# Attention and a gated feed-forward layer: outer weight units by chunk, weights split on GpSimd and copies on ScalarE in batch 0, end rows paired off chip

## The chip, the cores and the metric

One core of a Trainium2 chip runs the kernel. Its engines are TensorE (PE, matmuls; the loading of its weights is shown as PEld), VectorE (DVE), ScalarE (ACT), GpSimd (POOL) and the DMA queue of SyncE (SP); the time is that of one execution on the device, in microseconds (us). A change counts as measured when it is over about 0.2%.

## What is computed

Attention with a soft cap on the scores for 4 batches of 12 heads, 448 rows of 64, and behind it a gated product with 1536 inner columns:

```python
scores = cap * tanh(q @ k.T / sqrt(64) / cap)
x = softmax(scores) @ v             # (4, 12, 448, 64) -> x of (1792, 768)
gate = 1 / (1 + exp(-(x @ w_gate)))  # w_gate, w_val of (768, 1536)
out = (gate * (x @ w_val)) @ w_out   # w_out of (1536, 768)
```

Everything is in 32 bits; the three weights come in 64 bits.

## The kernel before

**Precision.** Each product of the feed-forward layer is made of three matmuls: an operand is split into a high part (a copy rounded to the type that TensorE takes, `hi`, line 207 on POOL, 209 on ACT, 211 on DVE) and a low part (the difference, `lo`, line 215), and the products high x low, high x high and low x high are added up in PSUM.

**Staging.** The attention runs in 24 steps of two heads (`_bounded_attention`), six to a batch. The feed-forward layer of a batch is `moe(b)`: a first product (24 units of weights, gate and value columns in turn, 18 matmuls of 448 columns a unit, line 893), and a second product (12 units, six for each half `t` of the output columns, line 984). The second product has the 384 full rows of the batch as 3 chunks of 128; a unit is 2 of the 12 inner blocks (`KU`), so 6 matmuls of 384 columns for each chunk, 18 for a unit. The 64 rows left in each batch (`REST`) go to DRAM (`grest`) and are gathered for the last batch, which works them as two more chunks of 128. While `moe(b)` runs, the attention of batch b + 1 is put between its matmuls; the two generators are advanced in turn by the amounts that they yield. Before that the attention of batch 0 runs alone, to about 70 us. By the trace batch 0 of the layer takes from 72 to 262 us, batch 1 to 431, batch 2 to 596, and batch 3, with no attention beside it, to the end.

**Order.** The orders of TensorE and ACT are those in which the program is written. Those of DVE, POOL and SP are made by the scheduler from priorities and a timeline of its own, and are then fixed; `tc.high_priority` moves an instruction ahead.

**Weights.** There are 36 units in a batch. In batch 0 they come in 64 bits (line 752) into three buffers, are converted to 32 bits by ACT (line 769) and three steps of DVE (lines 770 to 772) into one of two `pair` buffers, and are split into one of four `wspl` buffers (`WB = 4`): the high part by ACT and the low part by DVE, but for the first four units both by POOL (`o.early = 4`). `next_w(u)`, called just before the matmuls of unit u, converts unit u + 4, splits unit u + 3 (`AHEAD`) and hands out unit u. Split units are stored in DRAM (`wd`, line 822) and loaded again in the batches behind (`load_to(u + WB)`, line 843, into the slot that unit u - 1 has left); twelve units of a batch (`whole`) are stored as 32 bits (`wr`, line 779) and split on chip each time. The first four units are stored from ACT's queue when they are used.

**PSUM.** The feed-forward layer has three tiles (tag `m`), which both products go round in. ACT's tanh (line 934) reads a gate tile, DVE (line 937) a value tile, POOL and DVE split the result (`gspl`); the second product's tiles are copied to SBUF with a factor 0.5 (line 1006 on DVE, 1008 on ACT) and go out from SP's queue (line 1011). In batches 0 to 2 all copies are DVE's; in batch 3 DVE and ACT take turns.

## Time and profile before

| | |
|---|---|
| median of three runs | 756.18 us (755.86 to 757.0) |
| profiled execution | 755.29 us, span 753.5 us |
| PE busy | 739.8 us, 3900 matmuls |
| PEld, DVE, ACT, POOL busy | 639.7, 506.5, 378.2, 217.1 us |
| mean granted TensorE clock | 0.997 of full speed |
| matmuls of the first product | 377.2 us |
| matmuls of the second product | 159.6 us on a batch's own rows, 26.6 on the gathered ones |
| DMA | 151.78 MB, mean 201 GB/s |

An engine's busy time is the time in which any of its instructions runs. A row of an instruction begins with its start and length in us; in square brackets stands how long its engine was idle before it and what ended that. A row of waits has the engine and line that waited, what it waited for, the sum in us, the times and the longest.

### The profile page before, as it was taken

The numbers are of one execution on the slowest core, as the hardware profiler recorded it, in microseconds if no ns is written. First come the engines' busy times: TensorE is split into PE (matmuls) and PEld (weight loads), VectorE is DVE, ScalarE is ACT, GpSimd is POOL, SyncE is SP. The second block draws the span as 40 slices with busy tenths as digits, with TensorE's granted clock in tenths as the row PEclk, the third lists the DMA queues.
The fourth block names the chain that finished last, engine by engine and source line by source line (L and its number), as shares of the span: only waits on it lengthen the run. The fifth ranks groups of instructions, "written<-read, shape, count | busy, mean of one in ns | idle before, by whom it ended". The sixth has DMA issues, their size and how long they took to land.

```text
span 753.5 us, 10326 instructions
## 1 busy us (share of the span) xinstructions
PE 739.8 (98%) x3900; PEld 639.7 (85%) x3900; DVE 506.5 (67%) x544; ACT 378.2 (50%) x418; POOL 217.1 (29%) x223
## 2 busy tenths in 40 slices
PE   8999999999999999999999999999999999999996
PEld 6556777777788888888899988988989999999996
DVE  2898688979999939988897638889877132322000
ACT  5997577767577346666564246665561011111000
POOL 1364001021211616463545305455552000000000
PEclk9999999999999999999999999999999999999998
DMA  5866898997899964444567954523379946463541
GB/s 125 224 151 157 294 324 249 319 282 257 259 266 383 310 200 150 106 157 134 165 185 247 296 166 151 142 102 113 126 195 308 335 152 187 148 194 99 184 159 57
DMA packets 133511, 151.78 MB, mean 201 GB/s; under 512 B 86860, under 2 KB 111948, under 8 KB 133452
## 3 DMA queue, kind: packets, MB, share of 16 engines
q1 hardware_dynamic: 130588, 147.02, 63.1%
q10 hardware_dynamic: 2864, 4.00, 1.5%
q8 instruction: 33, 0.54, 0.3%
q14 instruction: 26, 0.21, 0.1%
HBM read 118.75 MB, written 31.46 MB: 199 GB/s over the span
## 4 chain that ended last, share of the span: by engine, by line
PE 82%; DVE 8%; DMA 3%; issue 2%; POOL 2%; ACT 1%; SPq 1%; ACTq 0%; POOLq 0%; DVEq 0%
PE h L893 43%; PE o L984 20%; PE sc L413 6%; PE pv L474 4%; PE pv L484 2%; PE pv L483 2%; DVE rd L530 2%; DVE pair L772 1%; PE tp L244 1%; PE pv L465 1%; DVE pair L771 1%; DMA qk<-in_k_dram 1%; PE tp L360 1%; DMA wd<-wspl 1%; DMA wspl<-wd 1%
## 5 line engine op out<-in xcount | busy, mean ns | idle before, releaser
L893 PE MATMUL h<-xspl,wspl 128*128 128x448 f32 x1728 | 377.2, 372 | 0.9 <-DVE osb L1006 0.9
L893 PEld LDWEIGHTS h<-xspl,wspl 128*128 128x128 f32 x1728 | 321.3, 188 | 42.7 <-issue 15.2
L984 PE MATMUL o<-wspl,gspl 128*128 128x384 f32 x864 | 159.6, 338 | 1.4 <-DVE gate L937 1.2
L984 PEld LDWEIGHTS o<-wspl,gspl 128*128 128x128 f32 x864 | 150.4, 188 | 6.4 <-issue 3.8
L207 POOL TENSOR_SCALAR gspl<-gate 128x448 fp32r<-128x448 f32 x48 | 42.8, 891 | 240.8 <-DVE gate L937 240.4
L416 ACT ACTIVATE t<-sc,scale 128x896 f32<-128x896 f32 (+1 forms) x90 | 85.9, 1002 | 32.2 <-PE sc L413 31.9
L209 ACT ACTIVATE wspl<-pair 128x768 fp32r<-128x768 f32 x68 | 57.5, 845 | 87.4 <-PE h L893 72.7
L937 DVE SCALAR_TENSOR_TENSOR gate<-gate,h 128x448 f32<-128x448 f32 x48 | 29.7, 618 | 84.8 <-PE h L893 70.3
L424 ACT ACTIVATE t<-t,capv 128x1792 f32<-128x1792 f32 (+2 forms) x48 | 83.3, 1738 | 0.8 <-issue 0.6
L215 DVE TENSOR_TENSOR wspl<-pair,wspl 128x768 fp32r<-128x768 f32 x68 | 74.5, 1095 | 3.3 <-ACT wspl L209 2.9
L530 DVE RECIPROCAL rd<-rd 128x448 f32<-128x448 f32 x24 | 70.7, 2947 | 5.5 <-ACT rd L503 2.7
L934 ACT ACTIVATE gate<-h 128x448 f32<-128x448 f32 x48 | 26.0, 543 | 92.0 <-PE h L893 91.3
L413 PE MATMUL sc<-T 64*128 64x448 f32 (+1 forms) x522 | 66.5, 382 | 1.1 <-DVE T L215 1.1
L413 PEld LDWEIGHTS sc<-T 64*128 64x128 f32 (+1 forms) x522 | 44.9, 181 | 20.7 <-issue 12.1
L1006 DVE TENSOR_SCALAR osb<-o 128x384 f32<-128x384 f32 x22 | 11.9, 554 | 61.0 <-PE o L984 60.9
L436 POOL TENSOR_TENSOR a<-t 128x448 f32<-128x448 f32 x24 | 31.7, 1323 | 70.3 <-ACT t L424 37.4
L209 ACT ACTIVATE ph<-t 128x1792 fp32r<-128x1792 f32 x24 | 40.8, 1699 | 14.5 <-PE pv L485 14.4
L215 DVE TENSOR_TENSOR pl<-t,ph 128x1344 fp32r<-128x1344 f32 x24 | 47.2, 1968 | 0.4
L215 DVE TENSOR_TENSOR gspl<-gate,gspl 128x448 fp32r<-128x448 f32 x48 | 38.5, 802 | 7.7 <-POOL gspl L207 7.4
L769 ACT ACTIVATE pair<-w 128x768 f32<-128x768 f32 x36 | 32.5, 907 | 19.1 <-DVE wspl L215 10.5
L772 DVE SCALAR_TENSOR_TENSOR pair<-w,pair 128x768 uint16<-128x768 uint32 x36 | 41.8, 1165 | 0.3
L474 PE MATMUL pv<-t,vo 112*128 112x448 f32 x96 | 40.1, 539 | 0.4 <-ACT t L424 0.4
(92 smaller groups left out, 721.4 us busy)
## 6 DMA issues: line engine op xcount, KB each, us to landing
wspl<-wd SPq DMA_DIRECT2D x72, 768.0 KB, 5.7
wd<-wspl SPq DMA_DIRECT2D x20, 768.0 KB, 5.3
pair<-wr SPq DMA_DIRECT2D x36, 384.0 KB, 3.1
w<-in_moe_w_gate_dram SPq DMA_DIRECT2D x12, 768.0 KB, 6.8
w<-in_moe_w_val_dram SPq DMA_DIRECT2D x12, 768.0 KB, 6.7
w<-in_moe_w_out_dram SPq DMA_DIRECT2D x12, 768.0 KB, 6.9
qk<-in_q_dram SPq DMA_DIRECT2D x44, 112.0 KB, 4.7
wr<-pair SPq DMA_DIRECT2D x12, 384.0 KB, 3.8
```

The source lines that it names most:

```text
L207: self.nc.gpsimd.tensor_scalar(dst, src, 1.0, 1.0, ALU.mult, ALU.mult)
L209: self.nc.scalar.activation(dst, src, AF.Copy)
L215: e.tensor_sub(dst, src, hi.bitcast(F32))
L413: nc.tensor.matmul(ps[0:w, j, 0:S], a[rows], r[rows], start=(i == 0), stop=(i == len(ops) - 1))
L416: nc.scalar.activation(Pt[n][0:w, :, m, :], ps[0:w, :, 0:S], AF.Tanh, scale=c["scale"][0:w])
L424: nc.scalar.activation(t, t, AF.Exp, scale=c["cap"][rows])
L474: nc.tensor.matmul(pv, vs[n][0:QC, j * NC + m, :], Pt[n][0:QC, j, m, :], start=(m == 0), stop=(m == NC - 1),)
L530: nc.vector.reciprocal(rd, rd)
L769: nc.scalar.activation(x, top.bitcast(F32), AF.Copy, scale=2.0 ** -112)
L772: nc.vector.scalar_tensor_tensor(half, low.bitcast(U32), 2.0 ** -29, half, ALU.mult, ALU.add)
L893: nc.tensor.matmul(ps, a, r, start=(kk == 0 and i == 0), stop=(kk == KD - 1 and i == 2))
L984: nc.tensor.matmul(ps, a, r, start=(y + kk == 0 and i == 0), stop=(y + kk == KF - 1 and i == 2),)
```

## The change

The high part of the weights goes from ACT to POOL for all units of batch 0 (`u < NU`), not the first four alone. Units 0 to 2 are stored in DRAM already in the attention steps 4 to 6 (`store_early`). The output copies are written behind each chunk (`copy_out`) and no longer behind all chunks; in batch 0 they are ACT's. In batches 1 and 2 the first two and the last two units of each half of the second product are worked together: for each chunk the matmuls of both units, then the next chunk; what prepares the units to come, for the second of the two, stands behind both. And the end rows of two batches lie beside each other in DRAM (`grest` of 128 columns), and the tiles that they are gathered in have those 128 columns innermost.

```diff
@@ -558,6 +558,8 @@
         live, last = n < NP, n == o.NPAIR
         if live:
             due = emit_S(n, 0) + emit_S(n, 1)
+            if NC <= n <= o.NPAIR:
+                o.store_early(n - NC)
             if n in PLAN:
                 o.convert_to(PLAN[n])
             yield due
@@ -809,7 +811,7 @@
         if u not in w_raw:
             return
         t, s = w_raw.pop(u), new_w(u)
-        o.hi("p" if u < o.early else "a", s[:, 0, :], t)
+        o.hi("p" if u < NU else "a", s[:, 0, :], t)
         o.lo("p" if u < o.early else "v", s[:, 1, :], t, s[:, 0, :])
         if u < KEEP or u >= o.early:
             w_spl[u] = s
@@ -870,18 +872,23 @@
 
     R, NR, KR = o.REST, B * o.REST, 3
     assert NR % P == 0
-    g_rest = []
-
-    def next_w(u):
+    g_rest, GR = [], P // R
+
+    def prepare_w(u):
         if u < NU:
             convert_to(u + LEAD)
         split_w(u + AHEAD)
         load_to(u + WB)
         load_raw_to(u + LEAD + 2)
-        w = w_spl.pop(u)
-        if u < KEEP:
-            store_w(u, w, nc.scalar)
-        return w
+
+    def store_early(u):
+        if u < KEEP and u not in w_dram:
+            store_w(u, w_spl[u], nc.scalar)
+
+    def next_w(u):
+        prepare_w(u)
+        store_early(u)
+        return w_spl.pop(u)
 
     def moe(b):
         u0 = b * NU
@@ -901,14 +908,16 @@
         if b == B - 1:
             tiles = []
             for tag, bufs, n in o.rest_tags:
-                r = ap.tile([P, n, 2, KR, NR], F32R, tag=tag, bufs=bufs, name=f"rest{len(tiles)}")
+                r = ap.tile([P, n, 2, NR // P, KR, P], F32R, tag=tag, bufs=bufs, name=f"rest{len(tiles)}")
                 tiles += [r[:, i] for i in range(n)]
             for x, r in enumerate(tiles):
-                for bb, d in enumerate(g_rest):
-                    nc.sync.dma_start(
-                        out=r[:, :, :, bb * R:(bb + 1) * R].bitcast(F32),
-                        in_=d[:, :, x * KR:(x + 1) * KR, :].bitcast(F32),
-                    )
+                for at, d in enumerate(g_rest):
+                    n = P if at < b // GR else b % GR * R
+                    for i in (range(2) if n < P else [slice(0, 2)]):
+                        nc.sync.dma_start(
+                            out=r[:, i, at, :, 0:n].bitcast(F32),
+                            in_=d[:, i, x * KR:(x + 1) * KR, 0:n].bitcast(F32),
+                        )
                 rest.append(r)
         u = u0
 
@@ -945,18 +954,21 @@
             lambda i, k, at=m * P: g_spl[:, i, k, at:at + P] for m in range(o.NF)
         ]
         if b < B - 1:
-            d = dram.tile([P, 2, KF, R], F32R, name=f"grest{b}")
-            nc.sync.dma_start(out=d.bitcast(F32), in_=g_spl[:, :, :, rest_cols].bitcast(F32))
-            g_rest.append(d)
+            if b % GR == 0:
+                g_rest.append(dram.tile([P, 2, KF, P], F32R, name=f"grest{b}"))
+            nc.sync.dma_start(
+                out=g_rest[-1][:, :, :, b % GR * R:(b % GR + 1) * R].bitcast(F32),
+                in_=g_spl[:, :, :, rest_cols].bitcast(F32),
+            )
         else:
             for x, r in enumerate(rest):
                 for i in range(2):
                     nc.sync.dma_start(
-                        out=r[:, i, :, b * R:].bitcast(F32),
+                        out=r[:, i, b // GR, :, b % GR * R:].bitcast(F32),
                         in_=g_spl[:, i, x * KR:(x + 1) * KR, rest_cols].bitcast(F32),
                     )
-            for at in range(0, NR, P):
-                chunks.append(lambda i, k, at=at: rest[k // KR][:, i, k % KR, at:at + P])
+            for at in range(NR // P):
+                chunks.append(lambda i, k, at=at: rest[k // KR][:, i, at, k % KR, :])
 
 
         for t in range(2):
@@ -966,16 +978,48 @@
                     acc.append(ps_m.tile([P, HM], F32, tag="m", name=f"o{b}_{t}_{m}"))
                 else:
                     acc.append(o.two_banks(f"o{b}_{t}_{m}")[:, 0, 0:HM])
+            dst_t = out[:, t * HM:(t + 1) * HM]
+            osr = None
             end = b == B - 1 and t == 1
+
+            def copy_out(m, ps):
+                nonlocal osr
+                if m == o.NF:
+                    tag, bufs = o.out_tag
+                    osr = ap.tile([P, NR // P, HM], F32, tag=tag, bufs=bufs, name=f"osr{b}_{t}")
+                if m < o.NF:
+                    dst = big.tile([P, HM], F32, tag="gate", bufs=3, name=f"osb{b}_{t}_{m}")
+                else:
+                    dst = osr[:, m - o.NF, :]
+                if end and m == len(acc) - 1:
+
+                    hm = HM // 2
+                    nc.vector.tensor_scalar(dst[:, 0:hm], ps[:, 0:hm], 0.5, None, ALU.mult)
+                    nc.scalar.activation(dst[:, hm:], ps[:, hm:], AF.Copy, scale=0.5)
+                elif m % 2 == 0 and b > 0 or 0 < b < B - 1:
+
+                    with tc.high_priority(offset=2 * AHEAD_OF):
+                        nc.vector.tensor_scalar(dst, ps, 0.5, None, ALU.mult)
+                else:
+                    nc.scalar.activation(dst, ps, AF.Copy, scale=0.5)
+                if m < o.NF:
+                    at = b * S + m * P
+                    nc.sync.dma_start(out=dst_t[at:at + P], in_=dst)
+
             by_chunk = KF - CLOSE * KU if end else KF
             x = 0
             while x < KF:
                 units = []
-                for y in range(x, KF if x >= by_chunk else x + KU, KU):
-                    units.append((y, next_w(u)))
+                if x >= by_chunk:
+                    to = KF
+                elif 0 < b < B - 1 and x in (0, KF - 2 * KU):
+                    to = x + 2 * KU
+                else:
+                    to = x + KU
+                for y in range(x, to, KU):
+                    units.append((y, next_w(u) if y == x or end else w_spl.pop(u)))
                     u += 1
-                x += len(units) * KU
-                for ps, g_of in zip(acc, chunks):
+                for m, (ps, g_of) in enumerate(zip(acc, chunks)):
                     for y, w in units:
                         for kk in range(KU):
                             wh, wl = (w[:, i, kk * HM:(kk + 1) * HM] for i in range(2))
@@ -985,32 +1029,14 @@
                                     ps, a, r, start=(y + kk == 0 and i == 0),
                                     stop=(y + kk == KF - 1 and i == 2),
                                 )
-                    yield 3 * KU * HM / S
-            to = out[:, t * HM:(t + 1) * HM]
-            for m, ps in enumerate(acc):
-                if m == o.NF:
-                    tag, bufs = o.out_tag
-                    osr = ap.tile([P, NR // P, HM], F32, tag=tag, bufs=bufs, name=f"osr{b}_{t}")
-                if m < o.NF:
-                    dst = big.tile([P, HM], F32, tag="gate", bufs=3, name=f"osb{b}_{t}_{m}")
-                else:
-                    dst = osr[:, m - o.NF, :]
-                if end and m == len(acc) - 1:
-
-                    hm = HM // 2
-                    nc.vector.tensor_scalar(dst[:, 0:hm], ps[:, 0:hm], 0.5, None, ALU.mult)
-                    nc.scalar.activation(dst[:, hm:], ps[:, hm:], AF.Copy, scale=0.5)
-                elif m % 2 == 0 or b < B - 1:
-
-                    with tc.high_priority(offset=2 * AHEAD_OF):
-                        nc.vector.tensor_scalar(dst, ps, 0.5, None, ALU.mult)
-                else:
-                    nc.scalar.activation(dst, ps, AF.Copy, scale=0.5)
-                if m < o.NF:
-                    at = b * S + m * P
-                    nc.sync.dma_start(out=to[at:at + P], in_=dst)
+                    if to == KF:
+                        copy_out(m, ps)
+                    yield 3 * (to - x) * HM / S
+                if to > x + KU and not end:
+                    prepare_w(u - 1)
+                x = to
             if b == B - 1:
-                ends = to.rearrange("(b s) e -> b s e", s=S)[:, o.FULL:]
+                ends = dst_t.rearrange("(b s) e -> b s e", s=S)[:, o.FULL:]
                 for bb in range(B):
                     m, r = divmod(bb * R, P)
                     queue = nc.scalar if t == 1 and bb == B - 1 else nc.sync
@@ -1019,7 +1045,7 @@
 
     MS = {mybir.EngineType.PE, mybir.EngineType.Activation}
     att = attention_of(o, x_done)
-    o.convert_to, o.load_weights = convert_to, begin_w64
+    o.convert_to, o.load_weights, o.store_early = convert_to, begin_w64, store_early
     first = big.tile([1, 1], F32, name="first")
     nc.scalar.activation(first, c["ident"][0:1, 0:1], AF.Tanh)
     with tc.manual_schedule(engines=MS):
```

## Rows read from the trace of the kernel before

**Rows 1.** The page: busy us (share of the span) and instructions of each engine.

```profile
PE 739.8 (98%) x3900; PEld 639.7 (85%) x3900; DVE 506.5 (67%) x544; ACT 378.2 (50%) x418; POOL 217.1 (29%) x223
```

**Rows 2.** The waits of TensorE from 60 to 600 us.

```profile
PE o L984 <- DVE gate L937: 1.2, 1, 1.2
PE tp L360 <- ACT t L416: 1.0, 1, 1.0
PE h L893 <- DVE osb L1006: 0.9, 1, 0.9
...
PE pv L474 <- ACT t L424: 0.4, 1, 0.4
...
PE o L984 <- DVE osb L1006: 0.2, 1, 0.2
```

**Rows 3.** Window: busy (x) of PE, PEld, DVE, ACT, POOL; clock, DMA share, GB/s.

```profile
70.00:262.00 192.00, 189.43 (x962) 154.35 (x958) 167.46 (x191) 127.93 (x150) 35.54 (x32) 1.00 0.91 292
```

**Rows 4.** The timeline of ACT, early in batch 0.

```profile
84.75 0.85 ACT L209 ACTIVATE wspl<-pair 128x768 fp32r<-128x768 f32 x1 [2.69 <-PE h L893]
...
85.50 3.46 ACT L424 ACTIVATE t<-t,capv 112x1792 f32<-112x1792 f32 x2
```

**Rows 5.** The timeline of ACT, where batch 0's second product begins.

```profile
209.00 0.85 ACT L209 ACTIVATE wspl<-pair 128x768 fp32r<-128x768 f32 x1 [3.06 <-DVE pair L772]
```

**Rows 6.** The timelines of ACT and DVE, where batch 0 ends.

```profile
260.94 1.91 ACT L416 ACTIVATE t<-sc,scale 128x896 f32<-128x896 f32 x2 [9.00 <-PE sc L413]
...
261.76 1.01 DVE L1006 TENSOR_SCALAR osb<-o 128x384 f32<-128x384 f32 x2
```

**Rows 7.** The timelines of DVE and PE, where batch 2's second product begins.

```profile
554.61 0.61 DVE L937 SCALAR_TENSOR_TENSOR gate<-gate,h 128x448 f32<-128x448 f32 x1
...
551.78 2.27 PE L984 MATMUL o<-wspl,gspl 128*128 128x384 f32 x12
555.28 2.38 PE L984 MATMUL o<-wspl,gspl 128*128 128x384 f32 x12 [1.23 <-DVE gate L937]
```

**Rows 8.** High parts of weights: ACT's (ns min/median/max) to 262 us, POOL's (mean).

```profile
L209 ACT ACTIVATE wspl<-pair x32: 830/847/862, 79.3 to 247.6; 128x768 fp32r<-128x768 f32 x32
...
L207 POOL TENSOR_SCALAR wspl<-pair 128x768 fp32r<-128x768 f32 x4 | 3.3, 834 | 4.0 <-DVE pair L772 4.0
```

**Rows 9.** The timelines of POOL and DVE in batch 0, splits that meet.

```profile
202.42 1.77 POOL L207 TENSOR_SCALAR xspl<-xraw 128x448 fp32r<-128x448 f32 x2
...
203.68 1.31 DVE L215 TENSOR_TENSOR wspl<-pair,wspl 128x768 fp32r<-128x768 f32 x1
...
173.24 2.21 POOL L207 TENSOR_SCALAR gspl<-gate 128x448 fp32r<-128x448 f32 x1 [8.85 <-DVE gate L937]
```

**Rows 10.** Timelines of POOL, DVE, SP and PE at the end of batch 0.

```profile
248.55 2.35 POOL L438 TENSOR_TENSOR a<-a,t 64x448 f32<-64x448 f32 x1
...
251.41 0.96 DVE L215 TENSOR_TENSOR wspl<-pair,wspl 128x768 fp32r<-128x768 f32 x1
252.29 2.95 DVE L530 RECIPROCAL rd<-rd 128x448 f32<-128x448 f32 x1
...
252.82 0.38 SPq L843 DMA_DIRECT2D wspl<-wd  x1
...
251.78 8.31 PE L984 MATMUL o<-wspl,gspl 128*128 128x384 f32 x47
```

**Rows 11.** DMA issues at 695 to 728, 392.6, 562 us: median us to landing.

```profile
wspl<-wd SPq DMA_DIRECT2D x7, 768.0 KB, 4.3
...
wspl<-wd SPq DMA_DIRECT2D x2, 768.0 KB, 6.1
...
wspl<-wd SPq DMA_DIRECT2D x2, 768.0 KB, 7.4
```

**Rows 12.** The timelines of SP and PE, late in batch 2's second product.

```profile
576.39 2.19 SPq L1011 DMA_DIRECT2D out_dram<-osb  x1
...
579.29 16.81 PE L984 MATMUL o<-wspl,gspl 128*128 128x384 f32 x96
```

More of the change, by code (lines that the diff above doesn't have):

```diff
@@ L968, in moe @@
                     acc.append(o.two_banks(f"o{b}_{t}_{m}")[:, 0, 0:HM])
+            dst_t = out[:, t * HM:(t + 1) * HM]
+            osr = None
             end = b == B - 1 and t == 1
-            by_chunk = KF - CLOSE * KU if end else KF
-            x = 0
-            while x < KF:
-                units = []
-                for y in range(x, KF if x >= by_chunk else x + KU, KU):
-                    units.append((y, next_w(u)))
-                    u += 1
-                x += len(units) * KU
-                for ps, g_of in zip(acc, chunks):
-                    for y, w in units:
-                        for kk in range(KU):
-                            wh, wl = (w[:, i, kk * HM:(kk + 1) * HM] for i in range(2))
-                            gh, gl = (g_of(i, y + kk) for i in range(2))
-                            for i, (a, r) in enumerate(((gh, wl), (gh, wh), (gl, wh))):
-                                nc.tensor.matmul(
-                                    ps, a, r, start=(y + kk == 0 and i == 0),
-                                    stop=(y + kk == KF - 1 and i == 2),
-                                )
-                    yield 3 * KU * HM / S
-            to = out[:, t * HM:(t + 1) * HM]
-            for m, ps in enumerate(acc):
+            def copy_out(m, ps):
+                nonlocal osr
                 if m == o.NF:
@@ L1010, in moe @@
                     at = b * S + m * P
-                    nc.sync.dma_start(out=to[at:at + P], in_=dst)
+                    nc.sync.dma_start(out=dst_t[at:at + P], in_=dst)
+            by_chunk = KF - CLOSE * KU if end else KF
+            x = 0
+            while x < KF:
+                units = []
+                if x >= by_chunk:
[6 more added lines that the diff above has]
+                    units.append((y, next_w(u) if y == x or end else w_spl.pop(u)))
+                    u += 1
+                for m, (ps, g_of) in enumerate(zip(acc, chunks)):
+                    for y, w in units:
+                        for kk in range(KU):
+                            wh, wl = (w[:, i, kk * HM:(kk + 1) * HM] for i in range(2))
+                            gh, gl = (g_of(i, y + kk) for i in range(2))
+                            for i, (a, r) in enumerate(((gh, wl), (gh, wh), (gl, wh))):
+                                nc.tensor.matmul(
+                                    ps, a, r, start=(y + kk == 0 and i == 0),
+                                    stop=(y + kk == KF - 1 and i == 2),
+                                )
+                    if to == KF:
[4 more added lines that the diff above has]
+                x = to
             if b == B - 1:
-                ends = to.rearrange("(b s) e -> b s e", s=S)[:, o.FULL:]
+                ends = dst_t.rearrange("(b s) e -> b s e", s=S)[:, o.FULL:]
                 for bb in range(B):
```

## The prediction

> **What bounds the kernel now.** I read the page's busy times first: TensorE (PE) is busy for 98% of the span [rows 1], so the span is nearly the sum of its matmuls, and the change takes none away. A matmul that waits for nothing runs at its pace, and 96 of the second product's stand in 16.81 us, 0.175 us each [rows 12]. So a gain can only come out of TensorE's waits, and the second view is the list of those, from 60 us (the attention head of batch 0 is over soon after) to 600 us (the last attention is over). It names five waits that the change could touch: 1.2 us for a gate of VectorE (DVE), 1.0 for a tanh of ScalarE (ACT), 0.9 and 0.2 for output copies on DVE, 0.4 for an exp on ACT [rows 2]. Together 3.7 us. Behind 600 us there is no such wait, and the first 60 us are not touched. That is the ceiling: 3.7 us of 755, if nothing new is late.
>
> **The change part by part.**
>
> **High parts of the weights, ACT to GpSimd (POOL), 32 instructions in batch 0.** ACT loses 32 x 0.847 us = 27 us, POOL gets 32 x 0.834 = 26.7 us [rows 8]; neither engine is full (128 and 36 us busy of 192 from 70 to 262 us) [rows 3], so the sums are worth nothing by themselves. What counts is that ACT runs in a fixed order and that this step sits in it, waiting for a weight slot or for a conversion. At 84.75 us it had waited 2.69 us for TensorE, and the exp that TensorE needed came out only at 85.5 [rows 4]: the 0.4 us. At 209.0 it had waited 3.06 us for DVE's conversion, and the tanh that frees a PSUM tile for the transposes stood behind it [rows 5]: the 1.0 us. With the step gone ACT reaches both early enough; next late would be ACT's conversion step, which waits for a pair buffer. I take both, 1.4 us.
>
> The price is on DVE. Where POOL reads SBUF beside a DVE step with two SBUF inputs, one of them is longer: the low part of a weight took 1.31 us at 203.68 beside POOL's splits [rows 9] where it takes 0.96 undisturbed [rows 10], 0.35 more; elsewhere POOL waited, its split of 448 columns lasting 2.21 us [rows 9]. A move costs DVE between 0 (POOL waits) and 0.834 us (the whole instruction). From 70 to 262 us DVE is busy 167.46 of 192 us [rows 3], so 24.5 are free, and the six copies that go to ACT free 6 x 0.55 = 3.3 more (two in 1.01 us) [rows 6]. Even 32 x 0.834 = 26.7 us stays below 27.8. I take 0.25 a move, 8 us in all (between the two rows, nearer to the one where POOL waits, because a split is released by DVE's own step and DVE goes straight on). It is covered as long as a weight is split three units before TensorE comes to it: 192 us for 36 units makes about 5 us a unit, so some 10 us.
>
> The rule in question is the Trainium skill's, "SBUF — State Buffer", section "Who interferes with whom": a DVE instruction with two SBUF inputs and a GpSimd instruction that reads SBUF exclude each other, and the second to start is held until the first is done. The trace agrees (0.35 us on DVE, or 2.21 us on POOL). Taken to its end the rule speaks against the move: every split would hold up somebody, and if it were always DVE the 24.5 us of room would be gone.
>
> Where the cover is thin is the end of batch 0. POOL is in the three adds of the attention until 248.55 + 2.35 = 250.9 us; the last unit's low part ran at 251.41, a reciprocal of 2.95 us right behind it, and the load of the next batch's first unit was issued at 252.82, behind the store that waits for that low part [rows 10]. TensorE needs that unit's low part 18 matmuls before the end of the 47 that end at 260.0, at 256.8 [rows 10]: 4.4 us of cover. A split behind the adds on POOL ends at 250.9 + 0.83 = 251.7, so the low part is done by 252.7 if DVE keeps its order: 0.3 us later, covered. The next batch's load then moves by 0.3 us as well. I book 0.3 and keep 0 to 2.2 (the rival below).
>
> **Output copies of batch 0 to ACT.** TensorE's 0.9 us at 262 is a PSUM tile whose copy DVE did only at 261.76, while ACT had been idle for 9.0 us before 260.94 [rows 6]. On ACT it is done when the matmuls end, and 0.85 + 0.2 us go. Against it: a copy now waits in ACT's order for its chunk and holds up what is behind it. That is a tanh or exp for matmuls that come later on TensorE too; and an exp of 1.8 us (two took 3.46 [rows 4]) ahead of the copy could bring back the 0.2 us. I book 1.1, between 0.8 and 1.1.
>
> **Two units by chunk at both ends of the second product, batches 1 and 2.** At 551.78 the first unit begins; the third chunk's PSUM tile was freed by the gate at 554.61 + 0.61 = 555.2, and TensorE came to it early, after 12 matmuls, and went on at 555.28 [rows 7]. With two units by chunk it comes after 24, 24 x 0.175 = 4.2 us, at 556.0. The 1.2 us go. At the other end the copies get more time, which no wait of these batches asks for.
>
> The price: both units are read until the last chunk, so their two slots come free together, and the units that refill them are asked for 36 matmuls, 36 x 0.175 = 6.3 us later, where before it was nine chunks, 9.4 us. A load took 4.3 us in quiet (7 of them), 6.1 us where two were issued together, 7.4 us beside the attention's last traffic and the gathering of the end rows [rows 11]. Besides, the queue of SP is in order: one issue of a copy took 2.19 us in this stretch instead of 0.34 or so [rows 12]. Between the two ends, -2.0 (in time) and +1.1 us late per place, the middle is on time by 0.2. There are four places without attention work between the matmuls (the second half, batches 1 and 2). I book 0.5 us in all, 0 to 6.3.
>
> **End rows paired off chip.** Twelve gathering loads stay twelve; by the shapes, four of them now move runs of 1536 bytes and eight half the bytes in runs of 256, where all were 256 on the side of SBUF. The tiles are read only in batch 3's second product, and no wait of TensorE names them [rows 2]. Nothing by itself; less traffic beside the loads above, which is why I take 0.5 there. **Three stores issued earlier** on ACT's queue, in the last attention steps before the first product: no instruction more; the bytes move out of a crowded stretch (DMA share 0.91 from 70 to 262 [rows 3]). Nothing, with 0.5 either way.
>
> **The sum.** 1.4 + 1.1 + 1.2 = 3.7 gained, 0.3 + 0.5 new: 2.9 less. The profiled execution took 755.29 us (span 753.5, 1.8 around it), so 752.4; the median of the runs, 756.18, lies 0.9 above it, so 753.3.
>
> **Rivals.** *POOL and DVE eat it at the end of batch 0.* If DVE's fixed order puts the reciprocal before the last low part: 251.7 + 2.95 + 0.96 = 255.6, the store, the load at 256.0, landing 6.1 later at 262.1. TensorE, 0.85 + 1.6 us earlier than before, would want it at 259.9 and wait 2.2 us. Left are 2.9 + 0.3 - 2.2 = 1.0: 755.2. For it: the thin cover, DVE full there; against: 251.41 shows the low part first. This is also where the skill's rule would bite first. *DVE saturated over all of batch 0* needs more than 0.87 us a move, above the whole instruction; it is out as an average.
>
> *Weights late (slower).* If each of the four places is late by the 1.1 us of the slow loads, and one issue by 1.9 more, TensorE waits 6.3 us for 3.7 gained less the 0.3: 759.1. It decides from 3.4 us on, about 0.85 a place, a landing 7.2 us behind the free slot. For it: 7.4 us was seen in just this stretch; against: 6.1 with two together, and fewer small packets.
>
> *The waits move.* The waits are short, and what was 0.3 us behind them (a conversion, a transposed tile, a copy behind an exp) takes their place: half the gain stays, 754.7 at most; the change does what it says and TensorE waits for someone else.
>
> **How the numbers follow.** Forecast 753.3, chance 0.52, own range 752 to 754.6. Rival at the end of batch 0: 0.15. Moved waits: 0.2, 754.5 to 756.5. Weights late: 0.13, 757 to 760. A measurement of this kernel tells about 0.2%, 1.5 us, from no change: faster is below 754.7. Faster: the forecast and a quarter to a half of the two middle cases, 0.64; same 0.25; slower 0.11. Range 751.8 to 757.2: below, the ceiling of 3.7 and 0.5 for the stores; above, a part of the late weights.
>
> **What would show it.** Right: of TensorE's waits from 60 to 600 us those for ACT's exp and tanh, the gate and the copies gone; the splits of weights on POOL at 0.83 to 2 us; ACT's copies right behind their chunks at 235 and 260. Wrong: waits of TensorE for loads of weights in the second halves of batches 1 and 2, or at the first unit of batch 1; DVE busy all through 230 to 262 with steps of 1.3 us and more where 0.96 stood; a first product of batch 1 that begins no earlier than 262.

## The result and the profile after

The changed kernel took 761.22 us (median of 8 runs, 759.2 to 762.51) beside 756.19 us for the one before: a ratio of 1.0057 with a 95% interval of [1.0047, 1.0068], so slower: by 5.0 us in the medians, by 4.3 as the ratio has it. The prediction was 753.3 us, faster, and its range ended at 757.2: wrong in sign and range. The profiled execution took 760.87 us, span 759.1. Below, "before" and "after" are the two kernels.

The page of after, engines (as [rows 1]):

```profile
PE 742.4 (98%) x3900; PEld 642.1 (85%) x3900; DVE 510.0 (67%) x538; ACT 356.1 (47%) x392; POOL 248.3 (33%) x255
```

The span is 5.6 us longer. 2.6 of it is *busy* time of TensorE, with the same 3900 matmuls; the other 3.0 is idle time. The waits of TensorE from 60 to 600 us in after (as [rows 2]):

```profile
PE o L1028 <- DVE wspl L215: 3.9, 1, 3.9
PE o L1028 <- DMA wspl<-wd: 1.8, 2, 1.3
PE o L1028 <- DVE gate L946: 0.6, 1, 0.6
PE tp L244 <- ACT t L416: 0.5, 1, 0.5
PE sc L413 <- DVE T L215: 0.2, 1, 0.2
```

All five waits of [rows 2] are gone, 3.7 us. In their place stand one wait of 3.9 us for a weight's low part, two for loaded weights (1.8), and one for a gate (0.6). The last two lines were there before. Two windows of after (us, then busy of PE, PEld, DVE, ACT, POOL, granted clock, DMA share, GB/s):

```profile
70.00:262.00 192.00, 187.04 (x943) 153.05 (x940) 172.13 (x186) 101.94 (x119) 62.26 (x61) 0.99 0.84 267
...
259.00:266.00 7.00, 6.28 (x24) 6.01 (x26) 2.54 (x4) 1.47 (x3) 0.56 (x1) 0.58 0.79 278
```

Beside [rows 3], ACT has 26 us less, POOL 26.7 more, and DVE 4.7 more although the copies left it. The second window is where the 2.6 us of longer matmuls are. The end of batch 0, timelines of PE, POOL and DVE in after (as [rows 10]), and last the same conversion step of DVE in before:

```profile
249.75 6.06 PE L1028 MATMUL o<-wspl,gspl 128*128 128x384 f32 x34
259.72 5.72 PE L1028 MATMUL o<-wspl,gspl 128*128 128x384 f32 x18 [3.91 <-DVE wspl L215]
...
248.27 1.74 POOL L437 TENSOR_TENSOR a<-a,t 128x448 f32<-128x448 f32 x1
250.09 1.75 POOL L438 TENSOR_TENSOR a<-a,t 64x448 f32<-64x448 f32 x1
252.89 1.98 POOL L207 TENSOR_SCALAR wspl<-pair 128x768 fp32r<-128x768 f32 x1 [1.06 <-PE o L1028]
...
244.63 1.04 DVE L774 SCALAR_TENSOR_TENSOR pair<-w,pair 128x768 uint16<-128x768 uint32 x1
...
250.86 1.89 DVE L774 SCALAR_TENSOR_TENSOR pair<-w,pair 128x768 uint16<-128x768 uint32 x1
...
254.21 1.13 DVE L215 TENSOR_TENSOR ph<-t,ph 64x448 fp32r<-64x448 f32 x1
...
255.92 2.94 DVE L530 RECIPROCAL rd<-rd 128x448 f32<-128x448 f32 x1
258.78 0.89 DVE L215 TENSOR_TENSOR wspl<-pair,wspl 128x768 fp32r<-128x768 f32 x1
...
245.62 1.86 DVE L772 SCALAR_TENSOR_TENSOR pair<-w,pair 128x768 uint16<-128x768 uint32 x1
```

Read it backwards. TensorE had done 34 matmuls by 255.8 and then stood 3.9 us for the last unit's low part, which DVE gave at 258.78 + 0.89 = 259.7. Before, it was ready at 252.4 [rows 10]. Ahead of it stood a reciprocal of 2.9 us, which came *behind* it in [rows 10]; ahead of that the last conversion, which ended at 250.86 + 1.89 = 252.75, in before at 245.62 + 1.86 = 247.48, 5.3 us earlier. It released POOL's split at 252.89 (the row names TensorE; but the slot that the split writes was that of unit 31, whose matmuls were over by 246, so it was the pair buffer that came last). Steps of DVE took 1.9 us beside POOL's adds where 1.04 stands without them; being later, three such steps on weights fell beside the adds instead of one (in before the attention's step `pl`, behind that one, was the long one: 2.51 us, against 1.55 in after). And the 18 matmuls behind the wait took 5.7 us, not 18 x 0.175 = 3.15: the granted clock in the window from 259 to 266 is 0.58, and from 258.0 to 264.8 the trace has half, the 1.2 GHz of the two levels. That is the 2.6 us of busy time.

The wait needs both, the late conversion and the new order. An estimate from these rows: in the old order the low part would have come behind the step `ph`, at 254.21 + 1.13 = 255.34 (POOL's split had ended at 252.89 + 1.98 = 254.87), and have been done at 256.3, 0.5 us after TensorE came for it instead of 3.9. No run forces the old order.

Why was the conversion late? The timelines of ACT's and SP's queues in after, 32 us earlier, and the time to landing of one of SP's issues (the columns are those of [rows 11]):

```profile
221.87 0.54 ACT L505 ACTIVATE xraw<-pv 64x448 f32<-64x448 f32 x1
224.87 0.46 ACTq L156 DMA_DIRECT2D v<-in_v_dram  x1
227.45 1.32 ACTq L161 DMA_DIRECT2D v<-in_v_dram  x2
228.82 1.80 ACT L424 ACTIVATE t<-t,capv 112x1792 f32<-112x1792 f32 x1 [6.41 <-issue]
...
219.06 0.56 SPq L824 DMA_DIRECT2D wd<-wspl  x1
219.72 0.37 SPq L754 DMA_DIRECT2D w<-in_moe_w_out_dram  x1
...
wd<-wspl SPq DMA_DIRECT2D x1, 768.0 KB, 5.8
```

ACT did nothing for 6.4 us with work at hand. It was to issue the loads of v, three transfers, and an issue waits in ACT's own order. Each transfer of this program counts its landing on a semaphore, and each of these issues of v waits until the earlier transfer on its semaphore has landed. The trace names the semaphores: in this stretch ten of them, 100 to 109, go round over the queues of SP and ACT. The first v load waits for 108, which had last belonged to the weight store issued at 219.06; that landed at 224.85, and the load went out at 224.87. The second waits for 109, which had belonged to the weight load of 219.72; that landed at 227.43, and the issue went out at 227.45. In the kernel before the scheduler had put SP's transfers in another sequence. Small loads of k had 108 and 109 and had landed by 220.83; only the third issue waited for a weight store (landed at 222.71, issue at 222.73). The same point of ACT's timeline has no gap:

```profile
221.49 0.42 ACTq L156 DMA_DIRECT2D v<-in_v_dram  x1
...
223.51 1.79 ACT L424 ACTIVATE t<-t,capv 112x1792 f32<-112x1792 f32 x1
```

Behind the gap stood an exp and a tanh of the attention and ACT's next conversion step (232.29 us); unit 32's conversion ended at 236.3, before at 232.5, and from there the conversions ended 3.3 to 3.8 us later, the last one 5.3. DVE's largest wait from 70 to 262 us, in before and then in after:

```profile
DVE pair L770 <- ACT pair L769: 14.5, 15, 2.3
...
DVE wspl L215 <- POOL wspl L207: 12.5, 12, 2.9
```

Before, DVE waited for ACT's conversion steps; after, for POOL's splits, whose low part stands next in its order. The sum is hardly different: more than half of DVE's idle time is time in which it waits in its order for a neighbour, and that part has only changed the neighbour.

Last, batch 2's second half, timelines of PE and of SP's queue in after:

```profile
588.16 7.58 PE L1028 MATMUL o<-wspl,gspl 128*128 128x384 f32 x42 [1.30 <-DMA wspl<-wd]
596.22 2.03 PE L1028 MATMUL o<-wspl,gspl 128*128 128x384 f32 x10 [0.49 <-DMA wspl<-wd]
...
582.16 3.72 SPq L917 DMA_DIRECT2D rest<-grest  x3
585.98 9.06 SPq L845 DMA_DIRECT2D wspl<-wd  x4
```

The loads for two units come out of SP's queue behind the gathering of the end rows, and TensorE waits for both.

So the ledger of the 5.6 us: -3.7 (the waits removed), +3.9 (low part), +2.6 (half clock behind it), +1.8 (loads), +0.6 (gate) make 5.2; 0.4 lies in small idle times outside these rows.

### The profile page after: what moved, and what is told of

Its sections match the earlier page's. It is cut to its first block, busy times and chain, and to the rows that moved or that the text cites. A ratio compares the mean times of both kernels' runs of the same rounds, so it can differ in the third digit from the quotient of the medians.

```text
span 759.1 us, 10351 instructions
## 1 busy us (share of the span) xinstructions
PE 742.4 (98%) x3900; PEld 642.1 (85%) x3900; DVE 510.0 (67%) x538; ACT 356.1 (47%) x392; POOL 248.3 (33%) x255
## 4 chain that ended last, share of the span: by engine, by line
PE 63%; DMA 2%; DVE 1%; SPq 0%; issue 0%; ACT 0%
PE h L900 35%; PE o L1028 17%; PE sc L413 4%; DMA wspl<-wd 2%; PE pv L484 2%; PE pv L483 2%; PE dn L522 1%; PE pv L485 1%; PE tp L360 1%; PE tp L244 1%; DVE rd L530 0%; SPq L845 0%; DVE ph L215 0%; DVE wspl L215 0%; DVE a L440 0%
## 5 line engine op out<-in xcount | busy, mean ns | idle before, releaser
L1028 PE MATMUL o<-wspl,gspl 128*128 128x384 f32 x864 | 162.8, 342 | 6.3 <-DVE wspl L215 3.9
L1028 PEld LDWEIGHTS o<-wspl,gspl 128*128 128x128 f32 x864 | 152.7, 190 | 12.2 <-DVE wspl L215 4.2
L215 DVE TENSOR_TENSOR wspl<-pair,wspl 128x768 fp32r<-128x768 f32 x68 | 76.9, 1132 | 15.0 <-POOL wspl L207 12.5
L207 POOL TENSOR_SCALAR wspl<-pair 128x768 fp32r<-128x768 f32 x36 | 35.5, 986 | 94.1 <-DVE pair L774 48.3
L209 ACT ACTIVATE wspl<-pair 128x768 fp32r<-128x768 f32 x36 | 30.4, 844 | 66.7 <-PE h L900 66.5
L1002 DVE TENSOR_SCALAR osb<-o 128x384 f32<-128x384 f32 x16 | 8.6, 555 | 62.8 <-PE o L1028 62.7
L215 DVE TENSOR_TENSOR gspl<-gate,gspl 128x448 fp32r<-128x448 f32 x48 | 41.3, 860 | 7.2 <-POOL gspl L207 6.9
```

What stands on the lines that cost most here:

```text
L207: self.nc.gpsimd.tensor_scalar(dst, src, 1.0, 1.0, ALU.mult, ALU.mult)
L209: self.nc.scalar.activation(dst, src, AF.Copy)
L215: e.tensor_sub(dst, src, hi.bitcast(F32))
L1028: nc.tensor.matmul(ps, a, r, start=(y + kk == 0 and i == 0), stop=(y + kk == KF - 1 and i == 2),)
```

## The experiments

Theory P: the splits on POOL cost the time, at the end of batch 0, by DVE's lateness and the clock behind it. Theory Q, its sharper form, tried further below: the lateness comes from ACT's stop at the v loads. Rivals: the pairs of units (late loads) cost it, or the copies on ACT. A ratio is against the kernel before, run beside on the same chip; its medians there lie between 755.94 and 756.23 us. The waits listed are TensorE's from 60 to 600 us if not said otherwise. Edits are to the kernel after if not said otherwise.

### Splits back on ACT

```diff
-        o.hi("p" if u < NU else "a", s[:, 0, :], t)
+        o.hi("p" if u < o.early else "a", s[:, 0, :], t)
```

> The changed kernel, but the high parts of weights in batch 0 are ACT's again (first four units POOL's, as before). Theory P, that the split on POOL makes the last low part of batch 0 late: the wait of TensorE for it (3.9 us in the changed kernel) goes, and with it the 6.8 us at half clock behind it, which make the 18 matmuls of the last unit 5.7 us long instead of 3.1 (2.6 us). 761.2 - 6.5 = 754.7, up to 756.1 if ACT's waits of the kernel before (1.4 us) come back. Rival S, that the copies on ACT or the early stores bring the delay: the wait stays, 760 to 761. Rival L, that the late loads of the paired units in batch 2 are the larger part: the wait for the low part may go, but the time stays over 758.5.

755.25 us, 0.9987 [0.9978, 0.9996], as expected. The clock stays whole from 60 to 600 us; the waits of TensorE from 60 to 600 us that matter:

```profile
PE o L1028 <- DMA wspl<-wd: 2.0, 3, 0.9
PE tp L360 <- ACT t L416: 0.9, 1, 0.9
```

The low part's wait and the gate's 0.6 are gone, the tanh's 0.9 is back. Six us hang on this one line; the rest of the change by itself is about 0.9 faster than before. The exp's 0.4 of [rows 2] is *not* back, though ACT has its splits again. What ACT waited for at 84.75 in before [rows 4] was a weight store of its own queue that still read the slot; the row names TensorE, but the chain of before has the store, landing at 79.30 + 5.36 = 84.66. With the stores issued early ACT's split there starts without a wait (the chain in before; the timeline of ACT in this run):

```profile
79.30 5.36 DMA wd<-wspl
...
82.89 0.83 ACT L209 ACTIVATE wspl<-pair 128x768 fp32r<-128x768 f32 x1
```

### Splits alone, in the kernel before

The same line of the kernel before is given `u < NU`.

> The kernel before with one part of the change alone: the high parts of all weights of batch 0 by POOL. Theory P: the wait for the last low part stands at the end of batch 0 and the clock falls behind it; 756.2 + 3.9 + 2.6 - 1.4 (ACT's waits that go) = 761.3, at least 759. Rival S: without copies on ACT and early stores the low part is in time; 754.8 to 756.2. A result of 757 to 759 would say that the delay of the low part has two sources.

760.61 us, 1.0056 [1.0043, 1.0069]: as much is lost with nothing but the splits. The waits:

```profile
PE o L984 <- DVE osb L1006: 5.2, 2, 3.0
PE o L984 <- DVE gate L937: 1.8, 2, 1.2
```

The time came as expected, the place did not: DVE is late already at the copies between the two halves, where the clock falls to half (240.2 to 247.0). With copies on ACT the same lateness shows at the last low part. ACT stands 7.5 us at the v loads here too.

### No pairs, and copies back on DVE

```diff
-                elif 0 < b < B - 1 and x in (0, KF - 2 * KU):
+                elif False:
```

> The changed kernel without the pairs of units in batches 1 and 2 (one unit after the other, copies written behind each chunk). Theory P: the pairs gave the 1.2 us for the gate of batch 2 and cost the two waits for loads in batch 2, 1.8 us; 761.2 + 1.2 - 1.8 = 760.6, between 760 and 761.5, and the waits for wspl loads are gone from the trace. Rival L: the loads cost more than their rows say (the waits hold up what stands behind them); under 759.5.

759.86 us, 1.0049 [1.0036, 1.0062], a little under the range. The loads' waits are gone, the gate's 1.2 is back, the low part stays:

```profile
PE o L1028 <- DVE wspl L215: 4.6, 1, 4.6
PE o L1028 <- DVE gate L946: 1.8, 2, 1.2
```

By the medians the pairs cost 1.4 us more than they bring, but this interval overlaps that of after, and the sum of the waits is about the same (6.4 us here, 6.3 there): by this run alone it is not shown.

The copies of batch 0 back on DVE:

```diff
-                elif m % 2 == 0 and b > 0 or 0 < b < B - 1:
+                elif m % 2 == 0 or b < B - 1:
```

> The changed kernel with the output copies of batch 0 on DVE again. If the lateness of DVE is one and the same and only shows where DVE is needed next, the wait for the last low part is replaced by a wait for the copies between the two halves of batch 0's second product (5.2 us in the run with the splits alone), the clock falls behind it, 760 to 761.5. If the copies on ACT are what made the low part late: 755 to 757.

760.89 us, 1.0059 [1.0046, 1.0073], the same as after: the lateness shows at the copies again (waits):

```profile
PE o L1028 <- DVE osb L1002: 4.1, 2, 2.9
```

### TensorE kept at work through the wait

22 matmuls with zeros for an operand (`o.zeros` is a part of a constant that the kernel has) are put before the last unit of batch 0; they add nothing to the sum.

```diff
+    o.zeros = ones[:, 0:D]
...
+                if b == 0 and t == 1 and to == KF and hasattr(o, "zeros"):
+                    for _ in range(22):
+                        nc.tensor.matmul(
+                            acc[0][0:P // 2], o.zeros, g_spl[:, 0, 0, 0:HM], start=False, stop=False
+                        )
```

> The changed kernel with 22 matmuls of zeros (64 columns of zeros against 384 columns, added to the first accumulator of batch 0's last unit) put on TensorE right before the matmuls that wait for the last low part: 22 x 0.175 = 3.85 us of work in place of the wait; the sum is not changed. If the idle 3.9 us are what lets the clock fall: the granted clock stays at 1.0 there, the last 18 matmuls take 3.1 us instead of 5.7, and the time is 761.2 - 2.6 = 758.6. If the clock falls for another reason, or the slow matmuls have another cause: 761 to 761.5.

762.63 us, 1.0087 [1.0068, 1.0105]: missed. The timeline of PE there, and further on:

```profile
255.58 3.97 PE L1025 MATMUL o<-gspl,ones 128*64 128x384 f32 x22
260.09 3.42 PE L1034 MATMUL o<-wspl,gspl 128*128 128x384 f32 x18 [0.54 <-DVE wspl L215]
...
285.35 0.47 PE L484 MATMUL pv<-pl,vs 128*128 128x448 f32 x1 [2.18 <-DVE pl L215]
```

At the place itself it went as said: 18 matmuls in 3.4 us instead of 5.7, and batch 1's first product began at 264.86, not 266.79. But these two microseconds were lost again, and as much besides: TensorE, now earlier, waited 2.2 us for a split of the attention at 285 (DVE had been waiting for the parts of v, whose load had gone out late from ACT's queue), with half the clock behind it from 286.2 to 289.7; a part of batch 1's first product that begins at 290.22 in after begins at 292.48 here. So at the end of batch 0 the fall of the clock hangs on the idle time, and its repair there is worth nothing while DVE and ACT are late.

### The v loads taken from ACT's queue

```diff
-            vnat[n] = o.load_v(n, nc.scalar if n < DIRECT + 2 else nc.sync)
+            vnat[n] = o.load_v(n, nc.sync)
```

> The changed kernel with the loads of v for the attention steps 12 and 13 issued on SP's queue instead of ACT's; the splits stay on POOL. Theory Q: ACT stood still for 6.4 us before 228.8 because its v loads waited for two unrelated transfers (a store of 768 KB landing at 224.85, a load of 768 KB), which use the same completion semaphore; so the conversions of the last units came 3 to 4 us late and with them the last low part. Then ACT's gap goes, TensorE waits less than 1 us for the last low part, the clock stays up: 761.2 - 3.5 - 2.6 = 755.1, between 754 and 756.5. Rival P (POOL's splits and DVE's fixed order by themselves): the wait is still 2.5 us or more and the time 759 to 761.

758.55 us, 1.0029 [1.0018, 1.0041]: about half of the loss, not all, and between the ranges of both theories. ACT's gap is gone, the clock is whole at the end of batch 0, but 1.5 us for the low part and 2.1 for loads stay (waits):

```profile
PE o L1028 <- DMA wspl<-wd: 2.1, 2, 1.7
PE o L1028 <- DVE wspl L215: 1.5, 1, 1.5
```

The edit has a cost of its own: SP, free to choose, sends these loads much too early, at about 24 us, and delays another of v, for which TensorE waits 1.7 us at 36 us. The same edit in the kernel before:

> The kernel before with the two loads of v on SP's queue, a control: ACT did not stand still there in the kernel before, so nothing is to be had. Theory Q: 755.8 to 756.8. If the v loads on ACT cost something in every kernel: under 755.5.

757.88 us, 1.0022 [1.0007, 1.0038], dearer than expected, by a wait at 36 us, with half the clock behind it to 42.8 (waits of its first 60 us):

```profile
PE pv L458 <- DMA vo<-in_v_dram: 2.0, 1, 2.0
```

The kernel before with the splits on POOL and this edit:

> The kernel before with the splits of batch 0 on POOL and the v loads on SP's queue; against the run with the splits alone (760.6) it shows what of that loss came through ACT's queue. Theory Q: the wait for the copies (5.2 us) shrinks to about 1 us or less and the half clock goes, 756 to 757.5; the rest of the loss, if there is one, is POOL's and DVE's. Rival P: 759.5 or more.

759.27 us, 1.0042 [1.0027, 1.0057]: missed. The wait at 36 us (1.7 us, and half the clock from 36.6 to 40.0) spoils the comparison; at the end of batch 0 it went as Q says, 1.8 us of waits for the copies instead of 5.2 and no fall of the clock. A cleaner edit holds the loads back: three writes of one element by ACT into the v tile, at the point where ACT issued the loads, and SP loads behind them.

```diff
+    def load_v(self, n, queue=None, hold=False):
...
+        if hold:
+            for r, m in ((0, 0), (0, self.NF), (self.REST, self.NF)):
+                self.nc.scalar.activation(
+                    v[r:r + 1, 0, m, 0:1], self.c["ident"][r:r + 1, 0:1], AF.Copy
+                )
...
-            vnat[n] = o.load_v(n, nc.scalar if n < DIRECT + 2 else nc.sync)
+            vnat[n] = o.load_v(n, nc.sync, hold=n < DIRECT + 2)
```

> The changed kernel with the two v loads on SP's queue, each held back by a one-element write of ACT (three writes a load), so that they are issued where ACT issued them and not at the start as in the three runs with v on SP, where TensorE waited 1.7 to 2.5 us at 36 us for another v load. Theory Q (ACT's queue stood still behind unrelated transfers): no gap of ACT at 222 to 229 us, the wait for the last low part 1.5 us or less as in the first run with v on SP, no half clock: 758.55 - 1.9 = 756.6, between 755.8 and 757.3. Rival P (POOL's split alone): 759 or more.

756.98 us, 1.0002 [0.9988, 1.0016], as expected: 4.2 of the 5.0 us are back. The waits, and DVE's timeline at the end of batch 0:

```profile
PE o L1033 <- DMA wspl<-wd: 3.0, 4, 1.2
PE o L1033 <- DVE wspl L215: 1.5, 1, 1.5
...
247.62 1.91 DVE L779 SCALAR_TENSOR_TENSOR pair<-w,pair 128x768 uint16<-128x768 uint32 x1
...
253.66 2.94 DVE L535 RECIPROCAL rd<-rd 128x448 f32<-128x448 f32 x1
256.52 0.89 DVE L215 TENSOR_TENSOR wspl<-pair,wspl 128x768 fp32r<-128x768 f32 x1
```

ACT's gap is gone. The last conversion ends at 247.62 + 1.91 = 249.53: of its 5.3 us of lateness 3.2 are gone and 2.1 stay. The reciprocal still stands ahead of the last low part, but 2.3 us earlier; TensorE waits 1.5 us and keeps its clock. The kernel before with the loads held:

> Control: the kernel before with the v loads on SP's queue, held back in the same way. Theory Q: nothing changes, 755.6 to 756.6; the wait at 36 us is not there.

755.06 us, 0.9985 [0.9971, 0.9998], a little faster than expected. In its trace the two waits for copies of [rows 2], 0.9 and 0.2 us, are gone, with the copies still on DVE: with the other edit its order came out otherwise here too. And the splits alone with the loads held:

> The kernel before with the splits of batch 0 on POOL and the v loads on SP's queue, held back. Against 760.6 (splits alone) and 756.0 (before) it parts the loss: Theory Q: waits of TensorE for copies and gate some 2 us more than before, no half clock in batch 0, less the 1.4 us of ACT's waits: 756.5 to 757.5. If all of the loss came through ACT's queue: 754.6 to 755.5. Rival P: 759 or more.

756.22 us, 1.0002 [0.9988, 1.0015], a little under the range. Splits alone were 760.61, so this edit takes back 4.4 us. But the same edit gave 1.0 us in the kernel before, where ACT had no gap. What hangs on ACT's standing behind the transfers, and on what follows from it, the half clock included, is therefore 3.4 to 4.4 us here and 3.2 to 4.2 in the changed kernel. What the splits cost without it is 756.22 - 755.06 = 1.2 us, with intervals that overlap.

### Versions that keep the good parts

Only units 4 to 27 on POOL (`u < 28`), so that the end of batch 0 is as before:

> The changed kernel with POOL splitting the units 4 to 27 of batch 0 and ACT the units 28 to 35. If only the last eight conversions matter, the cover of some 10 us takes up all that POOL's splits cost before: no wait for a low part over 0.5 us, 754 to 755.5. If the delay builds up over all of batch 0: over 757.5.

758.79 us, 1.0038 [1.0025, 1.0052]: missed. ACT's gap, which lies earlier, is still there, and the wait behind it moved to ACT's own copies (timeline of ACT; waits of TensorE):

```profile
229.65 1.79 ACT L424 ACTIVATE t<-t,capv 112x1792 f32<-112x1792 f32 x1 [6.47 <-issue]
...
PE o L1028 <- ACT osb L1004: 3.2, 1, 3.2
```

The clock is at half behind this wait too, from 238.8 to 245.7. So it is not the splits of the last eight units that bring the delay. Splits on ACT and one pair only, the first of the first half (`0 < b < B - 1 and t == 0 and x == 0`), where the gate's 1.2 us were:

> The changed kernel with the splits on ACT again, and of the pairs only the first one of the first half in batches 1 and 2 (where TensorE waited 1.2 us for the gate, and where attention between the matmuls gives the loads more time). Theory: the gain for the gate stays and the three waits for loads in batch 2 (2.0 us in the run with the splits on ACT and all pairs) go: 755.25 - 2.0 = 753.3, at most 754. If the loads are late for another reason than the pairs (the end rows gathered on SP's queue): 755 or more.

753.0 us, 0.9955 [0.9942, 0.9969], as expected: faster than both kernels. Neither loads nor gates are waited for; of ACT's waits the tanh's is left:

```profile
PE tp L360 <- ACT t L416: 1.0, 1, 1.0
```

Against the first experiment, 755.25, the other three pairs of a batch cost 2.25 us, clear of the intervals; 2.0 of it are the waits for loads. The same with the copies on DVE:

> The kernel that came out at 753.0 (splits on ACT, one pair) with the output copies of batch 0 back on DVE: the price of that part alone. From the waits of the kernel before: 0.85 + 0.2 us more, 754.0; if the copies on ACT were worth nothing, 753.0.

754.14 us, 0.9977 [0.9968, 0.9986], as expected: the copies on ACT are worth 1.1 us. What is left of the change here (first pair, early stores, paired end rows) makes 1.8 us against before; the gate's 1.2 and the exp's 0.4 are the waits that went. Splits to unit 27 on POOL, one pair, v loads on SP, not held:

> A version meant to take every gain: POOL splits units 4 to 27 and ACT units 28 to 35, v loads on SP's queue, one pair of units (first half of batches 1 and 2 only), copies of batch 0 on ACT. Theory Q: none of the new waits is left, ACT's wait at 211 us (1.0 us) is gone too: 753.0 - 1.0 = 752.0, up to 752.8. If POOL's splits cost by themselves: 753.5 or more.

755.78 us, 0.999 [0.9977, 1.0002]: missed. No wait over 0.6 us from 60 to 600, but 2.5 us at 36 us for v, and half the clock behind it. The same with the loads held:

> The version meant to take every gain, without its wait at the start: POOL splits units 4 to 27, ACT units 28 to 35, one pair of units (first half of batches 1 and 2), copies of batch 0 on ACT, v loads on SP's queue held back. In the run before, no wait of TensorE over 0.6 us was left between 60 and 600 us. Theory Q: 755.8 - 1.9 - up to 1.7 of half clock = 752.2 to 753. If POOL's splits cost by themselves even where they are covered: over 753.5.

752.64 us, 0.9943 [0.992, 0.9965], as expected, the fastest seen, and level with the version of 753.0 within their intervals. TensorE's longest wait is

```profile
PE o L1033 <- DVE gate L951: 0.6, 1, 0.6
```

## Why the prediction was wrong

**Right.** That TensorE's waits set the time, and that the five of [rows 2] would go: they went. One for another reason than booked: the exp's 0.4 was a wait for a weight store, and with the stores early it goes without the splits; the prediction read [rows 4] by the name in the bracket and held the stores to be worth nothing. The copies on ACT: 1.1 booked, 1.1 measured. DVE's lengthening by the splits, 0.25 us a move and 8 us in all: DVE's busy time over the whole run is 514.7 us with the splits alone against 506.5 in before, and 510.0 in after against 500.9 with the splits back on ACT, so 8.2 and 9.1 us. The Trainium skill's page "SBUF — State Buffer", section "Who interferes with whom", says that a DVE instruction with two SBUF inputs and a GpSimd instruction that reads SBUF contend for a port that one holds at a time; the trace agrees at the end of batch 0, 1.9 us a step of DVE beside POOL's adds where 1.04 stands alone.

**The step that failed** is "0.3 us later, covered ... I book 0.3 and keep 0 to 2.2", for the end of batch 0. It was wrong in four points.

- *DVE keeps its order.* The step took DVE's order from [rows 10] with the reciprocal behind the last low part. That order is made anew from the whole program, and it came out the other way; the rival had named just this, at 0.15. By the estimate above that makes 3.4 of the 3.9 us once the conversion is late; without ACT's stop the same order leaves a wait of 1.5 us, where the run with the splits back on ACT, its last conversion nearly as late (249.38) but the old order kept, has none.
- *All else on time.* The step let the last conversion end at its old time. It ended 5.3 us later: 3.2 of that go when the v loads leave ACT's queue, where ACT had stood 6.4 us behind transfers of SP's queue, and that because SP's sequence had changed. No row among those of before shows such a stop, and I asked of ACT only what it computes. By the held loads, less what they give in before, this carries 3.2 to 4.2 of the 5.0 us. The other 2.1 us of lateness are no matter of the splits alone: with the splits back on ACT 1.9 are there too.
- *Busy time for cover.* "Some 10 us" set DVE's busy sum against its free time. But 14.5 of the free 24.5 us were waits for ACT's conversions, and after 12.5 are waits for POOL's splits: DVE could not use them to catch up, and ACT's delay stayed at 3.3 to 3.8 us over units 32 to 34 and went on to the end of the batch. By itself this swap of waits is no loss that the runs show: with the loads held it is there as well (12.6 us) and 4.2 us are back.
- *What late costs.* The rival's price was the next batch's load, 2.2 us. TensorE waited 3.9 us for the low part itself, and then paid 2.6 us more by the clock; the clock was in no term. The rows of before could not price it: its clock falls only at 749.7 us, behind the last matmul (747.8), which is what makes the page's mean of 0.997. Its place and mechanism were near, its price too small by a factor of three.

**A term too small:** the pairs' loads, booked at 0.5 us, measured as 1.8 us of waits in after and as 2.25 us for three of the four pairs. The bound of 6.3 held it; I took the middle of it from quiet loads, where the rows of SP's queue show a load behind the end rows. The first pair's wait for the gate, 1.2, went as said: it is the three other pairs that have nothing to gain and the loads to pay.

**Not shown:** the earlier stores and the paired end rows were not tried by themselves; the stores' 0.4 is read from the traces, and for the end rows about 0.2 of the 1.8 us above is left. How much of ACT's 6.4 us another sequence of SP would leave was not tried except by moving the loads, and the old order of DVE was not forced in any run; how the loss parts between stop and order stays open, as each makes the other dearer.

## What to carry to other kernels

Work moved to an idle engine changes the sequence of every queue that a scheduler fills; look, in each queue that computes and also issues transfers, for what an issue would have to wait. Ahead of the end of a phase ask of the last units, one by one, what stands before them on each engine in order, and price a wait of TensorE with the clock that it costs behind it. A change with several parts is worth taking apart: here one line lost 6 us, three of four pairs 2, and what was left was 3 us faster than before. And a row names one releaser: where the engine named had long been done, ask what else held the buffer, a store of it above all.

## What the runs showed of the hardware

TensorE's granted clock fell to half in an idle time of 3.9 us and stayed there to 264.8 us, and the 18 matmuls behind the wait cost 2.6 us more; filled with 22 matmuls and 0.5 us idle the same place kept the whole clock (1.00 in the window from 259 to 266), and it did so behind a wait of 1.5 us as well. The length of the wait alone did not decide it: at 36 us a wait of 1.7 us was followed by half the clock in the kernel before with the splits on POOL and v on SP, and not in the changed kernel with v on SP. Two issues on ACT's queue went out 0.02 us after unrelated transfers of 768 KB from SP's queue had landed (224.87 after 224.85, 227.45 after 227.43), and ACT, which had an exp to do, stood still until the last of its three issues was out.
